# Local attention and a gated MLP on one core: two heads' logits in one matmul, q and k in a ring, and a new order of the work

## The chip, the core and the metric

One Trainium2 chip, one of its cores. The metric is device time in microseconds, the median of a few runs. The core has a matrix engine (TensorE, PE in the profile), a vector engine (VectorE, DVE), an activation engine (ScalarE, ACT), a general engine (GpSimd, POOL) and a queue that issues transfers (SyncE, SP). They run side by side and wait for each other with semaphores. Matrix products go to PSUM, eight banks of 512 fp32 columns on 128 partitions. ACT and DVE carry them from there to SBUF.

## The reference, cut to what matters

```python
B, S, D = 1, 2048, 448; H = 16; Dh = 28; W, dil = 8, 2; Fh = 896
def _A_ref(x, wqkv, wo):                       # dilated local attention
    q, k, v = split_heads(x @ wqkv)
    idx = pos[:, None] - (arange(W) * dil)[None, :]     # the keys s, s-2, ..., s-14
    logits = einsum('bhsd,bhswd->bhsw', q, k[idx]) * Dh ** -0.5
    attn = softmax(where(idx >= 0, logits, -1e9))
    return einsum('bhsw,bhswd->bhsd', attn, v[idx]) @ wo
def _B_ref(x, w_in, w_sp, b_sp, w_out):        # gated MLP that mixes tokens
    z = gelu(x @ w_in); z1 = z[..., :Fh]; z2 = layernorm(z[..., Fh:])
    g = einsum('ts,bsf->btf', w_sp, z2) + b_sp[None, :, None]
    return (z1 * g) @ w_out
h = x + _A_ref(layernorm(x), ...); out = h + _B_ref(layernorm(h), ...)
```

Everything is bf16 in and out, 2048 tokens of 448 channels.

## The kernel before

**Stages.** Each of the 16 tiles of 128 tokens is loaded to x_tm. DVE makes its statistics (L625, L627), POOL the root (L619, L620), and DVE the normalized tile xn (L636). It is transposed to xhT: tiles 0 to 3 on PE with an identity (L665, copied out by ACT), the others by a DMA transpose (dma_T). From xhT PE makes q and k (jobs qk, five parts of tokens in the list QT, four groups of four heads each), with heads padded from 28 to 32 rows in the weights wqk, and v (jobs v, two blocks at a time). Attention runs over 18 blocks of queries (GEOM: 128, then 112 or 114 tokens, with 14 or 16 earlier keys). For a block PE makes the logits of 16 heads (jobs lg, L785), ACT the exponentials E (L797, L798), DVE sets all but the eight wanted keys to zero (L807), PE multiplies with v (jobs oA and oB, L820; a column of ones gives the sums), and DVE divides (L837, L840) into otm. A DMA transposes otm to OT, in some blocks by way of OTs and a copy (oc). PE projects 256 tokens with wo (jobs y), DVE adds x (L749) and the second layer norm follows, transposed to hnT. Then come the two halves of z (L496 again: z2 with a layer norm, z1), the mixing product with w_sp (L949), the gate (L958, L961), the last projection (L973), the sum (L980) and the stores. The line L506 is a helper for copies and L496 one for products in two halves A and B; their tiles tell the jobs apart.

**Tiles of the array.** Products with L496 and L820 use 64 rows by 128 columns of the array, two side by side. The logits of a block use 28 rows by 64 columns: 32 matmuls of 64 columns, in two jobs of 16, lg0 for partitions 0 to 63 and lg1 for 64 to 127. The second waits until the first has ended, and another job stands between them.

**Order.** Every piece of work is a job with what it reads and writes. ORDER is a list of all jobs' numbers, written out, that sets the order on each engine's queue; the number of the job "warm" in it places filler matmuls. BANK lists the PSUM bank of each ticket (a piece of PSUM that a product holds until it is carried out), and ON the engine for jobs that can run on ACT, DVE or POOL. Each queue is served in order. SP issues all loads, transposes and stores.

**Memory.** qkT holds q and k of all 2048 tokens; the upper half of w_sp (wsp_hi) comes into the same place later. V1 and E lie where the lower half's second part (wsp_lb) comes later.

Of the kernel before, what the change touches and what calls it, by code (L numbers as in the profile page):

```python
# [1048 lines left out]
```

## Time and profile before

| what | value |
|---|---|
| median of three runs | 246.53 us (243.91 to 248.43) |
| the profiled execution | 245.12 us |
| its span, first to last instruction | 243.4 us |
| mean granted clock of TensorE | 0.993 |
| PE, DVE, ACT, POOL busy | 96%, 60%, 34%, 14% of the span |

The span in slices shows three parts. Up to some 23 us data arrive and the first products start. Up to some 122 us attention, projections and z run mixed, with all engines in use. From there to 230 us PE runs the mixing product and the last projection alone, and some 13 us of tail follow. Times in rows of the timeline are microseconds from the span's start; a row gives start, busy time, engine, line, operation, tiles and, in brackets, how long the engine stood idle before it and for whom.

### The profile page before, as it was taken

Reading aid. Unit: us, or ns where it says so; the run is one execution under the profiler, and the core shown is the slowest. Engines: PE = TensorE matmul, PEld = TensorE weight load, DVE = VectorE, ACT = ScalarE, POOL = GpSimd, SP = SyncE. Lnnn points to the kernel's source line nnn. Section 1 sums busy time; section 2 is a strip of 40 time slices with the busy share of each in tenths; the row PEclk is TensorE's granted clock in tenths of the full one; section 3 lists DMA queues with packets and bytes.
Section 4 is the critical chain, followed back from the end, with each engine's and each line's share of the span. In section 5 each row is a group of like instructions: output and inputs, shape, how many; then the busy total and the mean of one; then the engine's idle time right before and its main releaser. Section 6 shows DMA issues by size and latency. Waiting matters only on the chain.

```text
span 243.4 us, 6131 instructions
## 1 busy us (share of the span) xinstructions
PE 233.3 (96%) x2688; PEld 120.4 (49%) x2688; DVE 146.5 (60%) x327; ACT 81.8 (34%) x99; POOL 33.4 (14%) x79
## 2 busy tenths in 40 slices
PE   7997997999999899999999999999999999999995
PEld 2674553556555455555544444444444444444443
DVE  7889862999788798898875014047313042633474
ACT  3778374372977259767740000000000000000000
POOL 6454020022121111231331000000000000000000
PEclk9999997999999999999999999999999999999999
DMA  6955757366488875859999940000000000012012
GB/s 207 345 167 112 107 108 142 90 99 159 88 135 88 116 130 107 108 119 196 203 179 238 198 84 3 0 0 0 3 19 0 0 0 4 0 38 95 21 38 94
DMA packets 66315, 23.34 MB, mean 96 GB/s; under 512 B 58608, under 2 KB 66160, under 8 KB 66288
## 3 DMA queue, kind: packets, MB, share of 16 engines
q1 hardware_dynamic: 66288, 22.95, 46.9%
q8 instruction: 21, 0.34, 0.6%
q14 instruction: 6, 0.05, 0.1%
HBM read 6.83 MB, written 1.84 MB: 36 GB/s over the span
## 4 chain that ended last, share of the span: by engine, by line
PE 78%; DVE 9%; DMA 7%; ACT 2%; issue 1%; POOL 1%; SPq 1%; POOLq 0%
PE psum L949 38%; PE psum L496 28%; PE psum L973 8%; DVE st L625 2%; DMA x_tm<-in_A_x_dram 2%; PE psum L820 2%; DMA OT<-otm 2%; DMA OTs<-otm 2%; DMA xhT<-xn 2%; DVE E L807 1%; DVE xn L636 1%; DVE ub L958 1%; ACT qkT L506 1%; DVE mv L627 1%; POOL rs L620 1%
## 5 line engine op out<-in xcount | busy, mean ns | idle before, releaser
L958 DVE TENSOR_TENSOR ub<-psum,bb 128x512 bf16<-128x512 f32 x28 | 19.3, 691 | 56.5 <-PE psum L949 56.0
L949 PE MATMUL psum<-wsp_hi,z2p 128*128 128x512 bf16 x224 | 50.3, 379 | 0.0
L949 PEld LDWEIGHTS psum<-wsp_hi,z2p 128*128 128x128 bf16 x224 | 21.9, 98 | 26.1 <-DVE ub L958 0.4
L496 PE MATMUL psum<-xhT,wqk 64*128 64x512 bf16 (+1 forms) x280 | 29.1, 339 | 0.7 <-DMA xhT<-xn 0.7
L949 PE MATMUL psum<-wsp_lb,z2p 128*128 128x512 bf16 x112 | 26.3, 379 | 0.0
L949 PE MATMUL psum<-wsp_la,z2p 128*128 128x512 bf16 x112 | 25.8, 379 | 0.0
L496 PE MATMUL psum<-w_in,hnT 64*128 64x448 bf16 x224 | 25.0, 349 | 0.0
L496 PE MATMUL psum<-hnT,w_in 64*128 64x512 bf16 x196 | 24.1, 376 | 0.0
L973 PE MATMUL psum<-w_out,z1p 128*128 128x448 bf16 (+1 forms) x119 | 22.7, 342 | 0.4 <-DVE z1p L961 0.4
L506 ACT ACTIVATE qkT<-psum 128x1024 bf16<-128x1024 f32 (+1 forms) x18 | 15.3, 859 | 16.1 <-PE psum L496 16.1
L625 DVE BATCH_NORM_STATS2 st<-x_tm 128x6 f32<-128x448 bf16 x32 | 19.5, 610 | 0.6 <-DMA x_tm<-in_A_x_dram 0.4
L884 DVE BATCH_NORM_STATS2 st<-z2p 128x6 f32<-128x448 bf16 x32 | 19.0, 610 | 1.2 <-ACT z2p L877 1.0
L798 ACT ACTIVATE E<-psum 128x1024 bf16<-128x1024 f32 x17 | 16.6, 1028 | 4.0 <-PE psum L785 3.8
L980 DVE TENSOR_TENSOR srg<-psum,x_tm 128x448 bf16<-128x448 f32 (+1 forms) x17 | 9.8, 593 | 13.0 <-PE psum L973 11.0
L949 PEld LDWEIGHTS psum<-wsp_lb,z2p 128*128 128x128 bf16 x112 | 11.0, 98 | 13.2
L949 PEld LDWEIGHTS psum<-wsp_la,z2p 128*128 128x128 bf16 x112 | 10.9, 98 | 13.3 <-DVE z2p L893 0.4
L496 PEld LDWEIGHTS psum<-xhT,wqk 64*128 64x128 bf16 x280 | 13.2, 95 | 8.5 <-issue 0.9
L620 POOL TENSOR_TENSOR rs<-rs,negh 128x2 f32<-128x2 f32 (+2 forms) x22 | 17.1, 776 | 1.8
L973 PEld LDWEIGHTS psum<-w_out,z1p 128*128 128x128 bf16 x119 | 11.5, 98 | 10.9 <-DVE z1p L961 0.9
L496 PE MATMUL psum<-wo,OT 64*128 64x448 bf16 x112 | 14.2, 367 | 2.5 <-DMA OT<-otm 1.8
L820 PEld LDWEIGHTS psum<-V,E 64*128 64x128 bf16 x576 | 12.3, 93 | 8.6 <-DVE E L807 1.9
L496 PEld LDWEIGHTS psum<-w_in,hnT 64*128 64x128 bf16 x224 | 11.3, 94 | 9.6 <-ACT OT L506 0.2
(61 smaller groups left out, 233.9 us busy)
## 6 DMA issues: line engine op xcount, KB each, us to landing
w_in<-in_B_w_in_dram SPq DMA_DIRECT2D x8, 224.0 KB, 3.6
out_dram<-srg SPq DMA_DIRECT2D x16, 112.0 KB, 1.7
x_tm<-in_A_x_dram SPq DMA_DIRECT2D x3, 448.0 KB, 6.2
wraw<-in_A_wqkv_dram SPq DMA_DIRECT2D x2, 448.0 KB, 4.2
w_out<-in_B_w_out_dram SPq DMA_DIRECT2D x1, 784.0 KB, 5.3
bb<-in_B_b_sp_dram SPq DMA_DIRECT2D x1, 512.0 KB, 5.4
wv<-in_A_wqkv_dram SPq DMA_DIRECT2D x2, 224.0 KB, 6.5
wo<-in_A_wo_dram SPq DMA_DIRECT2D x1, 336.0 KB, 7.7
```

Source lines behind the costliest of these rows:

```text
L496: ins = e.matmul(out(k), w(k, p0, c), x(k, p0, c), start=(k, p0, c) in first, stop=(k, p0, c) in last, tile_position=(p0, 0))
L506: j = pl.job(name, eng, key, [(lambda e: e.activation(o(), i(), AF.Copy) if eng == "act" else e.tensor_copy(o(), i()), list(reads), list(w ...
L620: (lambda e: e.tensor_tensor(R, A, negh[:, 0:1].to_broadcast([128, n]), ALU.pow), [rr, r_negh], r_rs[k][m:m + n])],
L625: [(lambda e: e.bn_stats(st[:, m, :], src), [rsrc], [r_st[k][m]])], dve_t(D))
L627: [(lambda e: e.bn_aggr(mv[:, m, :], st[:, m, :]), [r_st[k][m]], [r_mv[k][m]])], 0.09)
L798: return e.activation(o[:, :, :, 0:64], psum[:, tk.b * 512:tk.b * 512 + 1024].rearrange("p (i h q) -> p i h q", i=2, q=64), AF.Exp, scale= ...
L820: ins = e.matmul(psum[:, c:c + DH + 1], E[64 * r:64 * r + 64, slot, a:a + 128], V1[64 * r:64 * r + 64, vs, 4 * (2 * k + gg) + hh, 0:DH + 1 ...
L884: [(lambda e, m=m, k=k: e.bn_stats(st3[:, m, k, :], z2p[:, m, D * k:D * (k + 1)]), [r_z2[m]], [r_st[2][m]])], dve_t(D))
L949: ins = e.matmul(psv(tk), z2p[:, s, 128 * fc:128 * fc + 128], w[:, 512 * (tc % 2):512 * (tc % 2) + 512], start=(s == 0), stop=(s == NB - 1))
L958: [(lambda e, tc=tc, s=s, tk=tk: e.tensor_tensor(ub[:, s, :], psv(tk), bb[:, 512 * tc:512 * tc + 512], ALU.add), [r_bb], [r_ub[s]])], dve_ ...
L973: ins = e.matmul(psv(tk, 0, c1 - c0), z1p[:, fc, 128 * m:128 * m + 128], w_out[:, fc, c0:c1], start=(fc == 0), stop=(fc == FC7 - 1))
L980: [(lambda e, m=m, s=s, tk=tk, c0=c0, c1=c1: e.tensor_tensor(srg[:, s, c0:c1], psv(tk, 0, c1 - c0), x_tm[:, m, c0:c1], ALU.add), [r_x[m]], ...
```

## The change

**Logits.** q is written twice, to qd: copy 0 holds the even heads of each group with the odd heads' rows zeroed, copy 1 the odd heads. k goes to kT alone. One matmul then takes 64 rows (two heads' k) against both copies of q, 2 x 64 columns, on 64x64 tiles of the array. A block has 16 such matmuls in one job, where it had 32 in two; block 0 keeps two jobs.

**Evacuation.** Where one pass carried q and k of a group out of PSUM, there are now a pass for k (job qe, L512) and the masked q (job qf): two passes on ACT with a column of zeros and ones as scale (L723), or on DVE one multiplication of double width (L726).

**Ring.** qd and kT hold 1592 tokens. The fifth part of q and k (tokens 1578 to 2047, 14 of them made a second time) is written over the first two parts, once the blocks that read those are done. The parts have other lengths: 256, 312, 512, 512, 470 columns. V1 lies elsewhere, and the masks are made for all partitions.

**Order.** ORDER, BANK and ON are new throughout. `'z2c3'`, `'z2c6'` and `'z2c7'` move from DVE to ACT, `'ve10'` as well.

```diff
-QT = [(0, 256), (256, 512), (512, 1024), (1024, 1536), (1536, 2048)]
+QT = [(0, 256), (256, 568), (568, 1080), (1080, 1592), (1578, 2048)]
...
-ORDER = [21, 44, 29, 27, 22, 25, 43, 30, 0, 45, 46, 1, 52, 28, 2, 120, 121, 53, 47, 48, 3, 23, 54, 55, 4, 122, 5, 6, 128, 124,
+ORDER = [21, 45, 22, 24, 0, 25, 1, 53, 2, 44, 54, 46, 47, 27, 3, 55, 121, 124, 23, 48, 131, 49, 56, 4, 59, 61, 926, 926, 926,
...
+            [("qd", [128, 4, 2, SL], BF16), ("kT", [128, 4, SL], BF16)],
...
+        pl.job("qmz", "dve", -58.5, [(lambda e: e.memset(qm[:], 0.0), [], [r_qm])] +
+               [(lambda e, p=p: e.memset(qm[p:p + 32, p // 32 % 2:p // 32 % 2 + 1], 1.0), [r_qm], [r_qm]) for p in (0, 32, 64, 96)], 0.35)
...
-                move("qe%d_%d" % (t, g), "act", lo / 112.0 + KEY["qe"] + KEY["qkg"] * g,
-                     lambda lo=lo, hi=hi, g=g: qkT[:, 2 * g:2 * g + 2, lo:hi],
...
+                move("qe%d_%d" % (t, g), "act", ekey, lambda n=n, a=a, g=g: kT[:, g, a:a + n], lambda n=n, tk=tk: psv(tk, 1, n),
+                     [], [r_qk[t][3 * g]] + [r_qk[o][3 * g] for o in also], evac_t(n), [tk], (tk, 1, 1))
...
+                def fa(e, i, n=n, a=a, g=g, tk=tk):
+                    return e.activation(qd[:, g, i, a:a + n], psv(tk, 0, n), AF.Copy, scale=qm[:, i:i + 1])
+
+                def fv(e, n=n, a=a, g=g, tk=tk):
+                    return e.tensor_tensor(qd[:, g, :, a:a + n], psv(tk, 0, n).unsqueeze(1).to_broadcast([128, 2, n]),
+                                           qm[:].unsqueeze(2).to_broadcast([128, 2, n]), ALU.mult)
...
-                    for g in range(4):
-                        for i in range(2):
-                            p = 32 * (2 * j + i)
-                            c = (tk.b + i) * 512 + (128 * g if b == 0 else 64 * (4 * j + g))
-                            for r in range(2):
-                                ins = e.matmul(psum[64 * r:64 * r + 64, c:c + wd], qkT[p:p + DH, 2 * g + 1, k0 + 64 * r:k0 + 64 * r + 64],
-                                               qkT[p:p + DH, 2 * g, t0 + u0 * r:t0 + u0 * r + wd], start=True, stop=True,
-                                               tile_position=(p, 64 * r))
+                    for g in gs:
+                        for r in range(2):
+                            c0 = (tk.b + r) * 512 + 2 * ps_ * (g - gs[0])
+                            for c in range(2):
+                                o = psum[64 * c:64 * c + 64, c0:c0 + 2 * ps_].rearrange("p (s q) -> p s q", s=2)[:, :, 0:wd]
+                                ins = e.matmul(o, kT[64 * r:64 * r + 64, g, ks + 64 * c:ks + 64 * c + 64],
+                                               qd[64 * r:64 * r + 64, g, :, qs + u0 * c:qs + u0 * c + wd], start=True, stop=True,
+                                               tile_position=(64 * r, 64 * c))
```

Three places of the new order. First PE ahead of the first output projection (`wo,OT`; `xhT,wqk` is q and k, `qkT` are logits, `V_82,E` one half of a block's outputs). Before, from the second half of block 2's outputs on:

```order
L820 MATMUL psum<-V_82,E 128x29 x16
L496 MATMUL psum<-xhT,wqk 128x512 x6
L785 MATMUL psum<-qkT 64x64 x64
L496 MATMUL psum<-xhT,wqk 128x512 x8
L820 MATMUL psum<-V_82,E 128x29 x16
L496 MATMUL psum<-xhT,wqk 128x512 x6
L820 MATMUL psum<-V_82,E 128x29 x16
L496 MATMUL psum<-xhT,wqk 128x512 x8
L785 MATMUL psum<-qkT 64x64 x64
L496 MATMUL psum<-wo,OT 128x448 x8
```

After, the last ten rows ahead of the projection, and its first (`qd,kT` are logits, `wv,xhT` is v; block 2's outputs lie nine rows further up):

```order
L502 MATMUL psum<-xhT,wqk 128x512 x8
L814 MATMUL psum<-qd,kT 64x128 x16
L502 MATMUL psum<-xhT,wqk 128x512 x14
L845 MATMUL psum<-V_81,E 128x29 x16
L502 MATMUL psum<-xhT,wqk 128x512 x6
L845 MATMUL psum<-V_81,E 128x29 x16
L502 MATMUL psum<-wv,xhT 128x448 x8
L845 MATMUL psum<-V_81,E 128x29 x16
L502 MATMUL psum<-wv,xhT 128x448 x6
L845 MATMUL psum<-V_81,E 128x29 x16
L502 MATMUL psum<-wo,OT 128x448 x8
```

Between block 2's outputs and the projection stood 28 q/k matmuls, 128 of logits and two halves of outputs; now 56, 64 wider ones, 14 of v and six halves. The logits of a block now stand alone, so PE goes to them 19 times where it went 8 times.

Second, ACT at the start (`wqk` are pieces of padded weights, `xhT` the copies of a transposed tile). Before:

```order
L506 ACTIVATE wqk<-wraw 128x2x8x28
L506 ACTIVATE xhT<-psum 128x2x128 x2
L506 ACTIVATE wqk<-wraw 128x2x4x28
L506 ACTIVATE xhT<-psum 128x4x128
L506 ACTIVATE wqk<-wraw 128x2x4x28
L506 ACTIVATE wqk<-wraw 128x2x8x28 x2
L506 ACTIVATE qkT<-psum 128x2x256 x2
```

After:

```order
L512 ACTIVATE wqk<-wraw 128x2x8x28 x2
L512 ACTIVATE wqk<-wraw 128x2x4x28 x2
L512 ACTIVATE wqk<-wraw 128x2x8x28
L512 ACTIVATE xhT<-psum 128x2x128 x2
L512 ACTIVATE xhT<-psum 128x4x128
L512 ACTIVATE wqk<-wraw 128x2x4x28
L512 ACTIVATE kT<-psum 128x256
L723 ACTIVATE qd<-psum,qm 128x256 x2
```

The first copy of xhT has moved from behind one piece of weights to behind five, and a group's one copy has become three passes.

Third, DVE where the tiles 2 and 3 are normalized (`xn`). Before, behind the statistics of tiles 2, 3 and 4:

```order
L625 BN_STATS st_62<-x_tm 128x6
L627 BN_AGGR mv_63<-st_62 128x2
L625 BN_STATS st_62<-x_tm 128x6
L636 TENSOR_SCALAR xn<-x_tm,mv_63,rs_68 128x512 x2
L625 BN_STATS st_62<-x_tm 128x6 x2
```

After, the same place, behind the statistics of tiles 2 to 8:

```order
L634 BN_STATS st_62<-x_tm 128x6
L636 BN_AGGR mv_63<-st_62 128x2
L645 TENSOR_SCALAR xn<-x_tm,mv_63,rs_68 128x512
L634 BN_STATS st_62<-x_tm 128x6
L645 TENSOR_SCALAR xn<-x_tm,mv_63,rs_68 128x512 x3
```

The xn of tiles 2 and 3 have moved behind the statistics of four more tiles.

More of the change, by code (lines that the diff above doesn't have):

```diff
@@ L405, in bass_sequential_preLN__sliding_local_dilated__mixer_gmlp__prompt_kernel @@
         negh = sb("negh", [128, 1], F32)
+        qm = sb("qm", [128, 2], F32)
         tscr = sb("tscr", [128, 2], F32)
@@ L411, in bass_sequential_preLN__sliding_local_dilated__mixer_gmlp__prompt_kernel @@
         NV = 6
-        (qkT, o_qk), (wsp_hi, o_wh) = region(
-            [("qkT", [128, 8, S_TOK], BF16)],
+        SL = 1592
+        (qd, o_qk), (kT, _), (wsp_hi, o_wh) = region(
+            [("qd", [128, 4, 2, SL], BF16), ("kT", [128, 4, SL], BF16)],
             [("wsp_hi", [128, NB, 1024], BF16)])
-        (wv, o_wv), (xhT, o_xh), (wqk, o_wp), (z1p, o_z1), (w_out, o_wout) = region(
-            [("wv", [128, 4, D], BF16), ("xhT", [128, 4, S_TOK], BF16), ("wqk", [128, 4, 8, 128], BF16)],
+        (wv, o_wv), (xhT, o_xh), (wqk, o_wp), (V1, o_v), (z1p, o_z1), (w_out, o_wout) = region(
+            [("wv", [128, 4, D], BF16), ("xhT", [128, 4, S_TOK], BF16), ("wqk", [128, 4, 8, 128], BF16), ("V1", [128, NV, NHEAD, 32], BF16)],
             [("z1p", [128, FC7, S_TOK], BF16), ("w_out", [128, FC7, D], BF16)])
-        (E, o_e), (V1, o_v), (wsp_lb, o_wl) = region(
-            [("E", [128, NE, ESL], BF16), ("V1", [128, NV, NHEAD, 32], BF16)],
+        (E, o_e), (wsp_lb, o_wl) = region(
+            [("E", [128, NE, ESL], BF16)],
             [("wsp_lb", [128, 8, 1024], BF16)])
@@ L431, in bass_sequential_preLN__sliding_local_dilated__mixer_gmlp__prompt_kernel @@
         r_xh = [[spot("xh%d_%d" % (m, i), o_xh, 4 * S_TOK * 2) for i in range(XEH.get(m, 1))] for m in range(NB)]
-        r_qk = [[spot("qk%d_%d" % (t, g), o_qk, 8 * S_TOK * 2) for g in range(4)] for t in range(len(QT))]
+        r_qk = [[spot("qk%d_%d" % (t, g), o_qk, 12 * SL * 2) for g in range(12)] for t in range(len(QT))]
         r_E = [spot("E%d" % i, o_e + i * ESL * 2, ESL * 2) for i in range(NE)]
@@ L693, in bass_sequential_preLN__sliding_local_dilated__mixer_gmlp__prompt_kernel, with make_qk @@
                      [W_qk[i]], [r_pad[(i, k, g)] for g in range(g0, g1)], {"act": 0.052 + n / 1200.0, "dve": 0.068 + n / 3840.0})
-        for t, (lo, hi) in enumerate(QT):
-            n = hi - lo
+        def make_qk(t, also=()):
+            lo, hi = QT[t]
+            n, a = hi - lo, lo if t < 4 else 0
             for g in range(4):
@@ L705, in bass_sequential_preLN__sliding_local_dilated__mixer_gmlp__prompt_kernel @@
                         lambda k, p0, c, lo=lo, hi=hi: xhT[p0:p0 + 64, c, lo:hi], n, tk, lambda part, rd=rd: rd)
-                move("qe%d_%d" % (t, g), "act", lo / 112.0 + KEY["qe"] + KEY["qkg"] * g,
-                     lambda lo=lo, hi=hi, g=g: qkT[:, 2 * g:2 * g + 2, lo:hi],
-                     lambda n=n, tk=tk: psum[:, tk.b * 512:tk.b * 512 + 1024].rearrange("p (k t) -> p k t", k=2)[:, :, 0:n],
-                     [], [r_qk[t][g]], evac_t(2 * n), [tk], tk)
+                ekey = lo / 112.0 + KEY["qe"] + KEY["qkg"] * g
+                move("qe%d_%d" % (t, g), "act", ekey, lambda n=n, a=a, g=g: kT[:, g, a:a + n], lambda n=n, tk=tk: psv(tk, 1, n),
+                     [], [r_qk[t][3 * g]] + [r_qk[o][3 * g] for o in also], evac_t(n), [tk], (tk, 1, 1))
+                name = "qf%d_%d" % (t, g)
+                eng = ON.get(name, "act")
+                def fa(e, i, n=n, a=a, g=g, tk=tk):
[3 more added lines that the diff above has]
+                                           qm[:].unsqueeze(2).to_broadcast([128, 2, n]), ALU.mult)
+                wr = [[r_qk[o][3 * g + 1 + i] for o in (t,) + tuple(also)] for i in range(2)]
+                ops = [(lambda e, i=i, fa=fa: fa(e, i), [r_qm], wr[i]) for i in range(2)] if eng == "act" else [(fv, [r_qm], wr[0] + wr[1])]
+                durs = {"act": 2 * act_t(n), "dve": dve_t(2 * n)}
+                j = pl.job(name, eng, ekey, ops, durs[eng], use=[tk], rel=(tk, 0, 1))
+                j.alts = durs
+        for t in range(4):
+            make_qk(t)
         o_jobs = {}
@@ L768, in bass_sequential_preLN__sliding_local_dilated__mixer_gmlp__prompt_kernel @@
             slot = b % NE
+            if b == 6:
+                make_qk(4, (0, 1))
             rq = []
             for t, (lo, hi) in enumerate(QT):
-                if lo < t0 + nq and hi > t0 - pad:
+                if (t == 4 if b >= 14 else t < 4 and lo < t0 + nq and hi > t0 - pad):
                     rq += r_qk[t]
@@ L774, in bass_sequential_preLN__sliding_local_dilated__mixer_gmlp__prompt_kernel, with f @@
             var = {0: 0, 16: 1, 14: 2}[pad]
[L775 to L787 removed]
+            off = 1578 if b >= 14 else 0
+            for j in range(2 if b == 0 else 1):
+                tk = Ticket(2)
+                gs = (2 * j, 2 * j + 1) if b == 0 else range(4)
+                def f(e, qs=t0 - off, ks=t0 - pad - off, gs=gs, ps_=128 if b == 0 else 64, tk=tk, wd=wd, u0=u0):
+                    for g in gs:
[6 more added lines that the diff above has]
+                                               tile_position=(64 * r, 64 * c))
                     return ins
                 lgs[(b, j)] = pl.job("lg%d_%d" % (b, j), "pe", b + KEY["lg"], [(f, rq, [])], 0.2, acq=tk, kind="L")
[L790 to L791 removed]
                 def f2(e, j=j, slot=slot, tk=tk, b=b):
@@ L801, in bass_sequential_preLN__sliding_local_dilated__mixer_gmlp__prompt_kernel @@
                                       act_t(8 * 78 if b == 0 else 1024), use=[tk], rel=tk, tbl="exp")
-            if b:
-                pl.apart.append((lgs[(b, 0)], lgs[(b, 1)]))
             def fm(e, slot=slot, wd=wd, var=var):
```

38 lines of the change are left out of this document (16 added, 22 removed), and 89 rows, old and new, of tables (BANK, ON, ORDER).

## The prediction

> **What bounds the kernel now.** I read the page first (busy time, the 40 slices), then the stretches, then the chain of waits and TensorE's timeline where it stood still.
>
> ```profile
> PE 233.3 (96%) x2688; PEld 120.4 (49%) x2688; DVE 146.5 (60%) x327; ACT 81.8 (34%) x99; POOL 33.4 (14%) x79
> PE   7997997999999899999999999999999999999995
> DVE  7889862999788798898875014047313042633474
> ACT  3778374372977259767740000000000000000000
> ```
>
> TensorE (PE) is busy for 96% of the span. VectorE (DVE) and ScalarE (ACT) are busy only in the first half. So whatever takes work or waits from PE counts one for one; work added to the other engines counts where PE comes to wait for it.
>
> ```profile
> 12.00:23.00 11.00, 9.29 (x246) 6.13 (x242) 9.85 (x28) 9.33 (x14) 5.86 (x14) 1.00 0.53 137
> 23.00:38.00 15.00, 13.34 (x332) 7.84 (x332) 10.87 (x27) 8.62 (x10) 1.90 (x3) 1.00 0.67 112
> 35.40:38.80 3.40, 1.61 (x74) 1.16 (x72) 1.92 (x5) 2.28 (x3) 0.63 (x1) 1.00 0.62 87
> 38.80:42.20 3.40, 3.40 (x36) 1.69 (x32) 0.02 (x1) 1.02 (x1) 0.00 (x0) 0.50 0.87 186
> 42.20:62.00 19.80, 19.80 (x484) 11.61 (x482) 18.08 (x41) 9.81 (x10) 3.13 (x7) 1.00 0.57 113
> 62.00:83.00 21.00, 19.94 (x545) 11.74 (x545) 16.50 (x39) 15.16 (x17) 3.70 (x7) 1.00 0.72 104
> 83.00:122.00 39.00, 39.00 (x402) 20.73 (x398) 35.06 (x82) 28.43 (x33) 8.97 (x19) 1.00 0.82 143
> 122.00:230.00 108.00, 108.00 (x512) 49.88 (x511) 38.68 (x74) 2.33 (x3) 3.06 (x6) 1.00 0.24 49
> ```
>
> The columns are the stretch, its length, busy time of PE, PE's weight loads, DVE, ACT and POOL, then the granted clock. From 83 to 230 us PE has no idle time at all, and the change leaves those matrix products alone. Everything it can win or lose lies before 83 us and in the tail. There PE waits 1.7 us before 23, 1.7 us before 38, 1.1 us between 62 and 83, and it runs at half clock from 38.8 to 42.2, which wastes 3.4 x 0.5 = 1.7 us.
>
> The profiled execution took 245.12 us, 1.7 more than its span of 243.4. The median of the runs shown, 246.53, is 1.4 above it. My sum is made against 245.1.
>
> **1. The logits on PE: 0.0, between -3.8 and +4.3.**
>
> ```profile
> 28.51 0.82 PE L496 MATMUL psum<-xhT,wqk 64*128 64x512 bf16 x6
> 29.16 0.37 PE L820 MATMUL psum<-V,E 64*128 64x29 bf16 x16
> 29.36 1.69 PE L496 MATMUL psum<-xhT,wqk 64*128 64x512 bf16 x14
> ...
> 31.11 0.82 PE L496 MATMUL psum<-xhT,wqk 64*128 64x512 bf16 x6
> 31.86 0.87 PE L785 MATMUL psum<-qkT 28*64 28x64 bf16 x64
> 32.66 1.04 PE L496 MATMUL psum<-xhT,wqk 64*128 64x512 bf16 x8
> ```
>
> The first number is the start, so starts are compared. Six products take 0.65 us when the next work has the same 64x128 tiles (28.51 to 29.16) and 0.75 when logits follow (31.11 to 31.86): the way into the logits' tiles costs 0.10. The 64 logits of two blocks take 0.80 with the way back. Before: 18 blocks at 0.40 is 7.2, and PE goes into the logits 8 times, 0.8: together 8.0 us.
>
> After, a block is 16 matmuls of 128 columns in four quarters of the array, in place of 32 of 64 columns.
>
> ```profile
> 31.93:31.96 0.03, 0.03 (x12) 1.00 0.21 25
> 31.96:32.00 0.03, 0.03 (x16) 1.00 0.14 17
> ```
>
> These stretches of 0.032 us, of the logits alone, see 12 and 16 matmuls in flight, four more each time: four run side by side in 0.032. Six 512-column products take 0.65, two side by side, so a column costs 0.65/3/512 = 0.42 ns, and 64 more columns lengthen a group of four to 0.059. A block is four groups, 0.24; 18 make 4.3 us. But the new order goes into the logits 19 times. At 0.10 in and, as I assume, as much out, that is 3.8, and the total 8.1. What the wider matmul saves, the way in and out takes back. No row shows 64x64 tiles. If changing to them were free, the term is -3.8; if only two of the four ran side by side, +4.3. I take the nearest row, the 32x64 tiles that the kernel has, for both. The 14 tokens computed twice cost 28 pairs x 14 columns x 0.42 ns = 0.2.
>
> [...]
>
> **2. The start: +1.0.** The rows are the page's on DMA issues (the last number is us to landing) and the timelines of PE, ACT and DVE.
>
> ```profile
> xhT<-xn SPq DMA_TRANSPOSE x12, 3.5
> ...
> 8.04 2.90 PE L496 MATMUL psum<-xhT,wqk 64*128 64x256 bf16 x50
> ...
> 23.16 1.04 PE L496 MATMUL psum<-xhT,wqk 64*128 64x512 bf16 x8 [0.66 <-DMA xhT<-xn]
> 5.64 0.58 ACT L506 ACTIVATE wqk<-wraw 128x448 bf16<-128x448 bf16 x1 [3.36 <-DMA wraw<-in_A_wqkv_dram]
> 6.13 0.64 ACT L506 ACTIVATE xhT<-psum 128x256 bf16<-128x256 f32 x2
> 10.37 0.81 DVE L636 TENSOR_SCALAR xn<-x_tm,mv,rs 128x512 bf16<-128x512 bf16 x2 [0.28 <-POOL rs L620]
> 15.81 0.61 DVE L625 BATCH_NORM_STATS2 st<-x_tm 128x6 f32<-128x448 bf16 x1
> 16.46 0.18 DVE L627 BATCH_NORM_AGGREGATE mv<-st 128x2 f32<-128x6 f32 x1
> 16.56 0.60 DVE L625 BATCH_NORM_STATS2 st<-x_tm 128x6 f32<-128x448 bf16 x1
> ```
>
> Now ACT makes one piece of the padded weights ahead of the first copy of xhT; after, five, some 2 us of them (about 0.5 for a large one, 0.3 for a half), so I put the first product near 9.2 instead of 8.04. DVE now normalizes tiles 2 and 3 at 10.37; after, four more pairs of statistics stand ahead, 0.75 each (15.81 to 16.56), and adding them up I get 13.4 (an estimate, like the times that follow). ACT's order has the copies of those tiles ahead of the last k and q of the first 256 tokens, so block 0's logits come at about 16.7. PE meanwhile lacks work. The product of the third part of q and k needs one more transpose (tile 8); its xn comes near 20.6, and with 3.5 us to land PE starts it near 24.4 instead of 23.16. It then lacks two blocks of logits (0.6), and has 56 more tokens (0.65) and half a block of outputs (0.2). Net +1.0; I take 0 to +2.
>
> **3. The first output projection: -3.5.**
>
> ```profile
> 35.58 0.93 PE L785 MATMUL psum<-qkT 28*64 28x64 bf16 x64
> 38.30 1.24 PE L496 MATMUL psum<-wo,OT 64*128 64x448 bf16 x8 [1.79 <-DMA OT<-otm]
> 33.80 4.36 DMA OT<-otm
> ```
>
> The last row is from the chain: the transpose takes 4.36 us to land. PE waits 1.79 us for the transposed outputs of block 2, and the half clock follows. From the second half of block 2's outputs PE now has 28 q/k products (3.0 us), 128 logits (1.6) and two halves of outputs (0.4, by 29.16 to 29.36), some 5.1, ahead of the projection; it needed 7.2 (31.11 to 38.30). After, it has 56 (6.0), 14 v products (1.3), four blocks of logits (1.7) and six halves (1.2), 10.2. The wait should go, with the 1.7 us of half clock behind it. Late next would be the transposes for the fourth part of q and k: tile 12 is issued behind three loads of w_in, and I see about 1 us of room.
>
> **4. Evacuations: +1.5.**
>
> ```profile
> L506 ACT ACTIVATE qkT<-psum 128x1024 bf16<-128x1024 f32 x11 | 11.2, 1025 | 13.7 <-PE psum L496 13.7
> L506 ACT ACTIVATE qkT<-psum 128x512 bf16<-128x512 f32 x7 | 4.2, 599 | 2.4 <-PE psum L496 2.4
> L506 ACT ACTIVATE xhT<-psum 128x256 bf16<-128x256 f32 x2 | 0.6, 372 | 0.0
> L506 DVE CAST qkT<-psum 128x1024 bf16<-128x1024 f32 x1 | 1.2, 1225 | 0.1
> L506 DVE CAST qkT<-psum 128x512 bf16<-128x512 f32 x1 | 0.7, 686 | 0.0
> ```
>
> One pass per group becomes a k pass and, on ACT, two masked q passes. ACT now spends 11.2 + 4.2 = 15.4 us on them. After: 12 passes of 256 columns (372 ns), 10 of 312 (some 420), 15 of 512 (599) and 11 of 470 (some 560), 23.8 us. With one v evacuation taken from DVE, ACT gains 9.3 us before 75 us. DVE gains three double q passes (1225 each) and six k passes, 7.3, and loses 3.0. A masked ACT pass has no row; I take the copy's time, and 0.05 more on 34 passes would be 1.7 us of ACT. ACT has the room: in the stretches shown above from 12 to 83 us it was busy 42.9 of 66.8 us. But a group's three passes (3 x 0.6) now last longer than its 14 products (14 x 0.107 = 1.5), so PE may wait for a bank between 24 and 42 us: +0.5, estimated. Between 42 and 70 the same DVE work falls into a shorter time; it was already busy 18.1 of 19.8 us: +1.0 on top of the 1.1 us of waits there. Without ACT's room the price would be up to the 9.3. From 83 to 122 ACT takes three copies of z2 from DVE, under 3.1 us by the 1024-column row, hidden: it was busy 28.4 of 39.
>
> **5. The tail: -0.5.**
>
> ```profile
> 233.37 1.49 PE L973 MATMUL psum<-w_out,z1p 128*128 128x448 bf16 x7
> 234.80 0.42 DVE L961 TENSOR_TENSOR z1p<-ub,z1p 128x512 bf16<-128x512 bf16 x1
> 235.28 5.49 PE L973 MATMUL psum<-w_out,z1p 128*128 128x448 bf16 x35 [0.42 <-DVE z1p L961]
> ```
>
> Seven matmuls now stand between the last gate product and a wait for DVE's last z1p. After, 13 stand there, 1.1 us more cover.
>
> **Sum:** 0.0 + 0.2 + 1.0 - 3.5 + 1.5 - 0.5 = -1.3, so 245.1 - 1.3 = 243.8 us.
>
> **The rivals.**
> - *The clock halves early.* In the stretch before the half clock PE was busy 1.61 of 3.40 us; with the new start I count about 1.4 of 3.4 between 13.5 and 16.9. Another 1.7 us would go: 245.5. Against it: PE then waits less at tile 8. [...]
> - *The wait moves instead of going.* The SP queue is served in order, and its transposes wait for xn and otm. If the fourth q/k part or the projection still waits as long, term 3 is lost: 245.1 + 2.2 = 247.3.
> - *ACT sets the pace* (slower). If between 20 and 70 us PE finds the banks of q unread each time, ACT's added 9.3 us come through and hide the old waits (-3.5): 245.1 + 9.3 - 3.5 = 250.9. It decides once ACT's waits for PE's q and k, 13.7 + 2.4 us now, fall below some 4. For it: a group's passes outlast its products. Against: v, logits and outputs stand between the products.
> - *Visits to the 64x64 tiles are cheap.* Then 243.8 - 3.8 = 240.0.
> - *The 64x64 tiles run two at a time:* the wider matmul saves nothing and the visits cost: 243.8 + 4.3 = 248.1.
>
> **Chances.** Forecast 0.36, clock 0.14, moved wait 0.14, ACT 0.12, cheap visits 0.20, two at a time 0.04. Two per cent (4.9 us) is about what a measurement can tell from no change. Against the median shown, faster by that means below 241.6: the cheap visits and some of the forecast's spread, 0.24. Slower means above 251.5: most of the ACT case and its spread, 0.11. Within: 0.65. The range is 239.5 (cheap visits) to 249.5, which leaves out the ACT case and the far ends.
>
> **What would show it.** Logits: starts of a block's 16 matmuls 0.06 apart by fours, some 0.1 lost at each end. Start: first q/k product after 9 us, PE idle between 13 and 17. Projection: no wait for OT, and clock 1.00 at 38 to 45. Evacuations: PE's waits for qd and kT under 2 us in all. I am wrong if the half clock stays, or if ACT's wait for PE nearly disappears.

## The result, and the profile after

| | time, median of the runs | against the kernel before, 95% interval |
|---|---|---|
| before, beside the changed kernel | 245.95 us (243.91 to 248.43, 15 runs) | |
| changed kernel | 243.02 us (241.62 to 244.48, 15 runs) | 0.9893 (0.9865 to 0.9920) |
| before, beside the second series | 245.19 us (242.53 to 248.59, 29 runs) | |
| changed kernel, a second series | 243.02 us (241.60 to 243.83, 12 runs) | 0.9933 (0.9900 to 0.9966) |

The ratios are of fast runs alone (a run over 1.5% above the fastest of its kernel is left out), so they are not quite the quotients of the medians. The change takes off 0.7 to 1.1%, less than the 2% that the prediction takes for the mark, but both intervals lie below 1. The profiled execution took 243.01 us, its span 241.3. It is compared with the 245.12 and 243.4 of before: -2.1 us.

The page of the changed kernel, busy time and slices:

```profile
PE 233.5 (97%) x2397; PEld 116.4 (48%) x2408; DVE 145.7 (60%) x332; ACT 93.8 (39%) x132; POOL 35.6 (15%) x83
PE   7869999999999999999999999999999999999995
ACT  3697898588876797797630000000000000000000
PEclk9997999999999999999999999999999999999999
```

TensorE (PE) is as busy as before with 291 recorded matmuls fewer. ScalarE (ACT) has 12 us more work, all in the first half. The low digit of the clock stands in the fourth slice, near 20 us; before it stood near 40. The stretches say more (length, then busy time of PE, weight loads, DVE, ACT and POOL, then the granted clock):

```profile
12.00:23.00 11.00, 9.03 (x120) 4.80 (x118) 9.54 (x28) 8.72 (x18) 5.16 (x14) 0.84 0.45 99
15.37:18.78 3.41, 1.67 (x30) 0.65 (x26) 3.41 (x11) 3.41 (x7) 1.50 (x4) 1.00 0.34 61
18.78:22.19 3.41, 3.41 (x44) 1.57 (x38) 2.87 (x9) 2.53 (x4) 1.70 (x7) 0.50 0.51 95
23.00:38.00 15.00, 15.00 (x288) 8.27 (x284) 10.14 (x22) 13.21 (x23) 2.60 (x5) 1.00 0.85 146
38.00:62.00 24.00, 24.00 (x546) 13.44 (x544) 21.67 (x48) 18.93 (x27) 4.36 (x8) 1.00 0.66 109
62.00:83.00 21.00, 21.00 (x440) 11.76 (x438) 18.04 (x44) 15.53 (x19) 3.56 (x9) 1.00 0.88 136
```

From 23 to 83 us PE has no idle time left. It had 1.7 us before 38 and 1.1 us between 62 and 83, and 3.4 us at half clock behind the first output projection. Now the half clock comes at 18.78, behind a stretch in which PE was busy for 1.67 of 3.41 us. The timelines of DVE and PE show the start, the first output projection and the tail:

```profile
6.89 0.80 DVE L512 COPY wqk<-wraw 128x448 bf16<-128x448 bf16 x1 [0.66 <-DMA wraw<-in_A_wqkv_dram]
7.61 0.72 DVE L645 TENSOR_SCALAR xn<-x_tm,mv,rs 128x512 bf16<-128x512 bf16 x2
...
10.07 1.81 PE L502 MATMUL psum<-xhT,wqk 64*128 64x256 bf16 x30
17.45 0.33 PE L814 MATMUL psum<-qd,kT 64*64 64x156 bf16 x8 [1.75 <-ACT qd L723]
27.00 1.90 PE L502 MATMUL psum<-xhT,wqk 64*128 64x512 bf16 x16
28.84 0.42 PE L814 MATMUL psum<-qd,kT 64*64 64x128 bf16 x16
29.19 1.69 PE L502 MATMUL psum<-xhT,wqk 64*128 64x512 bf16 x14
...
44.93 0.92 PE L502 MATMUL psum<-wo,OT 64*128 64x448 bf16 x8
...
230.56 8.13 PE L998 MATMUL psum<-w_out,z1p 128*128 128x448 bf16 x49
```

The account of the profiled execution. The third part of q and k starts at 27.00 instead of 23.16, 3.8 later; about 0.25 of that is work (56 more tokens and half a block of outputs, two blocks of logits fewer, by the prediction's prices), 1.7 the half clock, and 1.9 the late first product and the wait at 17.45. Behind it 4.9 us are won by the start of the mixing product (120.84 instead of 122.10): the wait of 1.79 for OT, the 1.7 us of half clock behind it, and 1.4 of others, of which the smaller waits between 62 and 83 us are 1.1. From there to the end another 0.8 goes: the last 49 matmuls run through, where a wait of 0.42 stood before; the other 0.4 isn't traced. 3.6 - 4.9 - 0.8 = -2.1.

The half clock is not in every execution. Of the first 15 runs of the changed kernel 11 show a mean clock of 0.99 (median 243.15) and 4 one of 1.00 (242.02). Of 29 runs of the kernel before, in the second series, 9 show 1.00 (244.0) and 11 show 0.992 or 0.993 (245.7), the rest others. At one clock or the other the changed kernel is ahead by 2 to 2.6 us, so the gain doesn't hang on it.

### The profile page after: what moved, and what is told of

Same layout as the page of the kernel before. It is cut to its first block, busy times and chain, and to the rows that moved or that the text cites. A ratio compares the mean times of both kernels' runs of the same rounds, so it can differ in the third digit from the quotient of the medians.

```text
span 241.3 us, 5610 instructions
## 1 busy us (share of the span) xinstructions
PE 233.5 (97%) x2397; PEld 116.4 (48%) x2408; DVE 145.7 (60%) x332; ACT 93.8 (39%) x132; POOL 35.6 (15%) x83
## 4 chain that ended last, share of the span: by engine, by line
PE 79%; DVE 13%; POOL 2%; DMA 2%; ACT 1%; issue 1%; SPq 1%; DVEq 0%
PE psum L974 40%; PE psum L502 25%; PE psum L998 9%; DVE st L909 5%; PE psum L845 3%; PE psum L814 3%; DVE st L634 3%; DMA wraw<-in_A_wqkv_dram 2%; POOL rs L629 1%; DVE xn L645 1%; DVE z2p L918 1%; DVE x_tm L775 1%; DVE mv L912 1%; DVE mv L636 1%; POOL rs L628 1%
## 5 line engine op out<-in xcount | busy, mean ns | idle before, releaser
L502 PE MATMUL psum<-xhT,wqk 64*128 64x512 bf16 (+3 forms) x280 | 29.4, 342 | 0.0
L502 PE MATMUL psum<-w_in,hnT 64*128 64x448 bf16 x224 | 24.7, 349 | 0.1
L502 PE MATMUL psum<-hnT,w_in 64*128 64x512 bf16 x196 | 24.3, 376 | 0.0
L825 ACT ACTIVATE E<-psum 128x1024 bf16<-128x1024 f32 x17 | 17.3, 1023 | 5.1 <-PE psum L814 4.8
L723 ACT ACTIVATE qd<-psum,qm 128x512 bf16<-128x512 f32 (+3 forms) x34 | 18.2, 592 | 1.8 <-PE psum L502 1.8
L502 PEld LDWEIGHTS psum<-xhT,wqk 64*128 64x128 bf16 x280 | 12.4, 96 | 8.7 <-DVE wqk L512 0.5
L502 PEld LDWEIGHTS psum<-w_in,hnT 64*128 64x128 bf16 x224 | 10.6, 94 | 10.7 <-DVE x_tm L775 0.6
L628 POOL TENSOR_SCALAR rs<-mv 128x2 f32<-128x2 f32 (+2 forms) x22 | 6.7, 303 | 60.4 <-DVE mv L636 41.0
L946 ACT ACTIVATE z1p<-psum 128x1024 bf16<-128x1024 f32 x14 | 14.0, 1020 | 4.1 <-PE psum L502 4.0
```

What stands on the lines that cost most here:

```text
L502: ins = e.matmul(out(k), w(k, p0, c), x(k, p0, c), start=(k, p0, c) in first, stop=(k, p0, c) in last, tile_position=(p0, 0))
L628: [(lambda e: e.tensor_single_scalar(A, mv[:, m:m + n, 1], EPS, ALU.add), r_mv[k][m:m + n], [rr]), (lambda e: e.tensor_tensor(R, A, negh[: ...
L723: return e.activation(qd[:, g, i, a:a + n], psv(tk, 0, n), AF.Copy, scale=qm[:, i:i + 1])
L825: return e.activation(o[:, :, :, 0:64], psum[:, tk.b * 512:tk.b * 512 + 1024].rearrange("p (i h q) -> p i h q", i=2, q=64), AF.Exp, scale= ...
L946: return e.activation(o, i, AF.Gelu_apprx_tanh)
```

## The experiments

The starts of some pieces of PE's work, in us, from the profiled execution of each kernel (the mixing product marks the end of the part that differs):

| kernel | first q/k | first logits | third part of q/k | first projection | projection at 60 | mixing | mean clock |
|---|---|---|---|---|---|---|---|
| changed | 10.07 | 17.45 | 27.00 | 44.93 | 60.45 | 120.84 | 0.993 |
| changed, again | 10.26 | 17.65 | 25.88 | 43.79 | 59.32 | 119.42 | 1.00 |
| narrow | 10.09 | 17.47 | 25.71 | 43.91 | 61.10 | 122.99 | 1.00 |
| narrow, again | 10.17 | 17.56 | 27.29 | 46.51 | 63.43 | 124.29 | 0.993 |
| narrow, shifted | 10.06 | 17.45 | 26.96 | 45.02 | 60.70 | 121.18 | 0.993 |
| flat | 10.15 | 17.53 | 26.94 | 43.83 | 58.33 | 118.24 | 0.993 |
| more ACT | 10.08 | 18.69 | 29.84 | 49.62 | 66.07 | 127.09 | 0.993 |
| start, first trial | 9.12 | 18.53 | 28.03 | 45.95 | 61.48 | 121.69 | 0.993 |
| start, second | 9.07 | 15.10 | 26.39 | 44.84 | 60.37 | 121.30 | 1.00 |
| start, third | 7.87 | 15.55 | 27.78 | 45.68 | 61.21 | 121.36 | 1.00 |
| q on DVE | 10.04 | 16.79 | 25.60 | 43.51 | 59.03 | 119.14 | 1.00 |

My theory behind the result was that the new order brings the gain and the width next to nothing. The rival: the width brings it.

**The width alone.** Three runs with narrow logits in the new order (narrow, narrow shifted, narrow again in the table).

```diff
-  for r in range(2):
-      for c in range(2): matmul(both copies of q, 2 x 64 columns)
+  for s in range(2):              # one copy of q each
+      for r in range(2):
+          for c in range(2): matmul(copy s of q, 64 columns)
```

> The changed kernel with each wide logits matmul cut into its two copies of q: a block has 32 matmuls of 64 columns on the same 64x64 tiles, in the same place of the same order; nothing else differs. Theory (the gain comes from the new order, the width brings next to nothing): a group of four now starts every 0.056 us and should start every 0.032, so a block grows from 4 x 0.056 = 0.226 to 8 x 0.032 = 0.256, 18 blocks by 0.5 us: 243.0 + 0.5 = 243.5, about 0.990 of before. Rival (the 2.9 us gained come from the wider matmul and the 291 matmuls fewer): the time goes back to that of before, 245.9, ratio 1.00. Half of it back (244.5) would mean that both count.

Measured: 246.11 us, 1.0015 of before (0.9971 to 1.0059). The gain is gone, as the rival said, and yet the table does not show a wider matmul's time: from the third part to the first projection the cut kernel loses 0.3 us against the changed kernel at the same clock (0.17 ahead of it at the one, 0.12 behind at the other). By the projection at 60 it has lost 1.8, 1.5 of that at two places of its timeline:

```profile
53.16 0.29 PE L815 MATMUL psum<-qd,kT 64*64 64x64 bf16 x13 [0.42 <-issue]
57.44 0.19 PE L815 MATMUL psum<-qd,kT 64*64 64x64 bf16 x1 [0.71 <-issue]
```

PE stops inside a block's logits, after 19 and after 31 of its 32 matmuls, and waits for nothing that the profile shows. Numbered from 0 in order of start (PE's recorded matmuls, weight loads and semaphore instructions together), it resumes at records 1985 and 2241, 256 apart. The timeline of the kernel before has such a stop at record 2753, three times 256 further:

```profile
66.56 0.23 PE L820 MATMUL psum<-V,E 64*128 64x29 bf16 x5 [0.20 <-issue]
```

The trace also has transfers of instructions in pieces of 16,384 bytes, 21 in this kernel. So I suspected PE's own code. The next two runs tell that apart from a bank or an operand.

```diff
-  filler: matmul of 512 columns
+  filler: 4 matmuls of 128 columns        # the code behind it lies 138 records later
```

> The kernel with each wide logits matmul cut in two (32 of 64 columns), with one more edit: a filler matmul of 512 columns is now four of 128, so TensorE's instructions after the start lie 138 further on (69 matmuls, each with a weight load), for the same filler time. In the cut kernel TensorE stood still for 0.61 and 0.90 us inside two blocks' logits with nothing to wait for, at its recorded instructions 1985 and 2241, exactly 256 apart; in the kernel before 0.37 us at number 2753, three times 256 further; and the profile has TensorE's code come in pieces of 16 KB, the next ready some 1.5 us after its transfer ends. Theory (the code comes too late where 256 instructions last under some 4.3 us): the stalls again sit at numbers 193 + 256k, but now at other matmuls; none at those two blocks, and likeliest where 256 instructions take under 4 us: near 36 and 69 us. Rival (a bank or an operand of those two blocks): the same two blocks stall by 0.6 and 0.9 again, at numbers 138 higher. Time in both cases 244 to 246.5.

> The kernel with each wide logits matmul cut in two, once more, nothing altered. If TensorE's stalls inside two blocks' logits come from its code arriving in pieces of 256 instructions, they come back at recorded instructions 1985 and 2241 (blocks 9 and 10 of the attention, 0.3 to 0.9 us), since the program is the same, and the median is again 1 to 1.5 us above that of the shifted program (244.8): 245.5 to 246.5. If they were a chance of one execution, no stall and 244 to 245.

Measured, shifted: 244.81 us, 1.0006 (0.9968 to 1.0044). The two blocks run through; no gap at any record 193 + 256k exceeds 0.2 us. That refutes the rival, but no other matmul stalls either, so the guess on where was wrong. Measured, repeated: 245.37 us, 1.0053 (1.0014 to 1.0093), so 0.6 us above the shifted kernel, not the 1 to 1.5 expected, with both stops back in the same places, the third at record 1217, where the first run had only 0.34 between two starts, and a fourth near record 3009 (PE's timeline):

```profile
41.01 0.82 PE L502 MATMUL psum<-xhT,wqk 64*128 64x512 bf16 x6 [0.99 <-issue]
55.76 0.29 PE L815 MATMUL psum<-qd,kT 64*64 64x64 bf16 x13 [0.42 <-issue]
59.76 0.19 PE L815 MATMUL psum<-qd,kT 64*64 64x64 bf16 x1 [0.43 <-issue]
74.16 0.93 PE L502 MATMUL psum<-w_in,hnT 64*128 64x448 bf16 x8 [0.34 <-issue]
```

The transfers beside the stops, from the trace's records of the instruction queue (us):

```
kernel          record  last 256 records took* piece transferred   PE resumed   behind the transfer
before            2753                   3.21   64.06 to 65.05          66.56                  1.51
narrow            1985                   5.95   49.95 to 51.63          53.16                  1.53
narrow            2241                   4.28   54.94 to 55.88          57.44                  1.56
narrow, again     1217                   5.85   38.12 to 39.06          41.01                  1.95
narrow, again     1985                   5.95   53.40 to 54.36          55.76                  1.40
narrow, again     2241                   4.00   57.46 to 58.49          59.76                  1.27
```

(* the stop included.) PE resumes 1.3 to 2.0 us behind the end of a transfer each time. The pieces at 49.95, 53.40 and 38.12 started 2.75, 3.6 and 3.0 us after the boundary ahead of them, those at 57.46 and 54.94 started 1.7 and 1.8 us after theirs. In the shifted kernel the pieces between 33 and 60 us started 0.1 to 1.4 us after theirs. In the kernel before it was 0.7, but there 256 records lasted only 3.2 us. In these rows a stop comes where a piece starts late, or where the code is used up very fast. Why a piece starts late isn't shown. The changed kernel, with 32 records per block of logits in place of 64, has no such stop in either profile. So my theory stands in the records, where the width's own time is 0.3 us, and falls in the median: without the wide matmul the new order is level with the kernel before, or a little behind, in all three runs.

What the stops cost can be read from the table. From the third part to the projection at 60 us the shifted kernel takes 33.7 us, the other two 35.4 and 36.1, so the stops take 1.7 and 2.4 us there. They do not explain the whole. The shifted kernel has none, and its median is still 1.8 us behind the changed kernel of the same series (244.81 against 243.02). And the intervals of the three ratios overlap, so a cost of the stops in the median isn't shown. Nor was a narrow kernel with an order of its own run: this order belongs to the wide logits, and what loses may be the pair of the two.

**The way into the logits' tiles** (flat).

```diff
-  16 matmuls: 64 keys x (2 x 64 queries) on 64x64 tiles, for both halves of the keys
+   8 matmuls: 128 keys x (2 x 64 queries) on 64x128 tiles
```

> The changed kernel with the logits on 64x128 tiles, the tiles of the products around them: a matmul takes all 128 keys of a block against the first half's queries, 8 matmuls a block in place of 16. The logits of the upper 64 keys are thereby those of other queries, so this attention isn't the reference's; all shapes and all other work stay. Theory (the way into and out of the 64x64 tiles costs 0.09 to 0.10 us each): 19 visits x 0.19 = 3.6 us go, 243.0 - 3.6 = 239.4, and six products followed by logits take 0.65 us instead of 0.75. If PE only waits more elsewhere instead, less. Rival (the tiles' change is free, and the 0.1 is the read of q or the first matmul's own time): no change, 243.0.

Measured: 239.87 us, 0.9806 (0.9753 to 0.9859). Five of its six runs have a clock of 1.00; at that clock it is 2.1 us ahead of the changed kernel (239.73 against 241.80), so about 1 us of the 3.15 between the medians is the half clock that comes less often here. A visit that took from 28.84 to 29.19 takes 0.23:

```profile
28.66 0.40 PE L813 MATMUL psum<-qd,kT 64*128 64x128 bf16 x8
28.89 1.69 PE L502 MATMUL psum<-xhT,wqk 64*128 64x512 bf16 x14
```

Matched piece by piece, ACT's work is 0.07 us ahead of the changed kernel at 27 us and 3.05 ahead at 75. Between them lie 16 visits, so one costs 0.19 (the 0.17 in the next expectation shares the 3.05 among 18). At the mixing product 2.6 are left, since a wait of 0.50 us for OT at 86 us takes some back, and 2.0 at the end of the span (239.3 against 241.3). The theory holds for the price of a visit; of the 3.6 us that it expected, some 2 arrive.

**Fewer visits.** Then merging three of the 19 should bring 0.5.

```diff
-  lg5  qk3_0B  lg4   ...  lg10  v10B y2A lg11 y2B  lg9   ...  lg16  y6B v16A  lg15
+  lg5  lg4  qk3_0B   ...  lg10  lg9  v10B y2A lg11 y2B   ...  lg16  lg15  y6B v16A
```

> The changed kernel with three of its 19 visits to the logits' tiles merged: the logits of block 4 come directly behind those of block 5, of block 9 behind block 10, of block 15 behind block 16 (and ACT's exponentials of 9 ahead of those of 11); no other work moves. Theory (a visit costs 0.17 us in and out, by the flat trial's 3.05 us for 18): 0.5 us less by 72 us, unless a bank is not free in time; about 242.5 at the end. Rival (the entry's 0.1 hides the first operands' read and merging frees nothing, or the merged logits wait for banks): 243.0 or more.

Measured: 245.05 us, 0.9974 (0.9937 to 1.0011). The rival: the logits that come earlier wait for DVE to empty their bank, 2.1 us in all, which costs more than the 0.5.

```profile
53.31 0.42 PE L774 MATMUL psum<-qd,kT 64*64 64x128 bf16 x16 [1.29 <-DVE otm L825]
69.80 0.42 PE L774 MATMUL psum<-qd,kT 64*64 64x128 bf16 x16 [0.79 <-DVE otm L825]
```

**The projection's wait alone, in the kernel before.**

```diff
-  lg7  y0A  qk3_3B  o4A  y0B  v6A  o4B  v6B      ACT: ex7  ex6
+  lg7  qk3_3B  v6A  y0A  o4A  y0B  o4B  v6B      ACT: ex6  ex7
```

> The kernel before with its first output projection put later in the order: the other half of a q/k product and the first half of a v product now stand ahead of it (some 1.5 us of products), and block 6's exponentials ahead of block 7's so that the v product's bank is free; the rest of the order and the narrow logits stay. Theory (order): the wait of 1.79 us for the transposed outputs shrinks to about 0.4 and the half clock behind it (1.7 us) goes, -2 to -3.1: 242.8 to 243.9, so the time of the changed kernel without its wide logits. Rival (the wait only moves to the next projection or to v, or the clock halves anyway): 245.9, no change.

Measured: 244.55 us, 0.9983 (0.9947 to 1.0020). Inside the trace the term is there: this execution started 1.21 us late (its weights landed later), and DVE's work is 1.21 behind that of before at 35 us and 1.25 ahead at 47, so 2.5 us were won, within the 2 to 3.1 expected. Then the second projection waits, since DVE makes the evacuation of v ahead of it:

```profile
39.45 0.92 PE L457 MATMUL psum<-wo,OT 64*128 64x448 bf16 x8
...
47.73 0.93 PE L457 MATMUL psum<-wo,OT 64*128 64x448 bf16 x8 [0.83 <-DVE V L467]
```

By 56 us it is 0.5 ahead, by the mixing 0.4. The half clock went (9 of 12 runs at 1.00 against 9 of 29), the rest was given back. An order gains as a whole: one wait alone gave only a part.

**ACT's room** (more ACT).

```diff
-  ops = [masked pass i for i in range(2)]      # on ACT
+  ops = [masked pass i for i in (0, 0, 1)]
```

> The changed kernel with the first masked pass of every group whose q is on ACT made twice (same source, same place, same values): 15 or so more passes of 256 to 512 columns, some 8 us of ACT, all between 11 and 66 us. Theory (ACT is covered: its waits for PE's q and k are still 4.8 us in all, and PE doesn't wait for banks behind 24 us): at most +1.5, most of it at the first logits, which wait for ACT's q (one more pass on each of four groups ahead of them, up to 1.5 us). Rival (ACT sets the pace): the 8 us come through, less the 4.8 of waits, +3 or more: 246 or more.

Measured: 249.59 us, 1.0227 (1.0179 to 1.0275): the rival. The 17 added passes are 9.9 us of ACT, and 6.6 of them come through. The groups of the page, first of this kernel, then of the changed one (instructions, busy us, mean ns):

```profile
L723 ACT ACTIVATE qd<-psum,qm 128x512 bf16<-128x512 f32 (+3 forms) x51 | 28.1, 588 | 1.4 <-PE psum L502 0.7
```

```profile
L723 ACT ACTIVATE qd<-psum,qm 128x512 bf16<-128x512 f32 (+3 forms) x34 | 18.2, 592 | 1.8 <-PE psum L502 1.8
```

PE's timeline in this kernel, and ACT's waits for q and k in the changed one (us in all, times, longest):

```profile
18.69 0.33 PE L814 MATMUL psum<-qd,kT 64*64 64x156 bf16 x8 [2.87 <-ACT qd L723]
29.04 0.37 PE L845 MATMUL psum<-V,E 64*128 64x29 bf16 x16 [0.42 <-ACT qd L723]
66.07 0.93 PE L502 MATMUL psum<-wo,OT 64*128 64x448 bf16 x8 [0.61 <-ACT qd L723]
```

```profile
ACT kT L512 <- PE psum L502: 3.0, 5, 1.6
ACT qd L723 <- PE psum L502: 1.8, 4, 1.0
```

1.2 us are lost at the first logits and the rest bit by bit up to 72 us. ACT's waits for q and k, 16.1 us before, are 4.8 in the changed kernel and 2.9 here. Of the 9.9 us added, 3.3 were absorbed: less than those 4.8, though ACT is idle for 61% of the span.

**The start.** Three trials, then one job. In the trials DVE normalizes tiles 0 and 1 ahead of the weights' copies, ACT gives up two to four weight pieces, and there are fewer fillers.

> The changed kernel with its start in another order: DVE normalizes tiles 0 and 1 ahead of the copies of weights that wait for their load, and tiles 2 and 3 ahead of most statistics of tiles 4 to 11; ACT copies xhT ahead of three weight pieces; two of ACT's weight pieces and one masked q go to DVE; fewer fillers. Everything after 25 us keeps its order. Theory (the start is a net loss of 3.6 us by the third part of q and k, 1.9 from the late first product and the wait for q, 1.7 from the half clock at 18.8): the first q/k product comes at 8.2 to 8.6 in place of 10.07, and PE has no stretch of 3.4 us that is half idle; the third part starts at 24 to 25.5, where the transpose of tile 8 (landed at 24.9) bounds it, in place of 27.0: 243.0 - 1.5 to 2.5 = 240.5 to 241.5. Rival (what is late at the start is hidden by later waits): no change, 243.0.

> The start in another order once more, mended: in the last trial DVE made the masked q of the last group, and had it at the end of a row of statistics; TensorE waited 4.2 us for it. Now DVE makes it directly behind the statistics of tile 7, and ACT carries k of that group ahead of the transposed tiles 2 and 3. Theory: first q/k product near 9.1 us as in the last trial (10.07 in the changed kernel), first logits near 15.5 in place of 17.45, no half clock behind, third part of q and k at 24.5 to 25.5 in place of 27.0; at the end -1 to -2.5 against the changed kernel, 240.5 to 242. Rival (later waits for transposes take it back): the third part starts earlier but the mixing product does not, 243.

> The changed kernel with its start put in order a third time. In the second trial TensorE's first logits came at 15.1 in place of 17.5, but it then waited 1.5 us for the transpose of tile 4, 1.3 for DVE to carry k out of the bank of the next v product, and a transfer was late at 88 us. Now: DVE takes two more weight pieces from ACT, a memset of E goes from DVE to POOL, tile 4 is normalized one statistic earlier, DVE carries the second part's k between statistics, and POOL makes no memset while DVE normalizes tile 0. Everything behind 25 us keeps its order. Theory (the start's loss can be recovered): first product near 8.0, first logits near 14, third part of q and k at 23.4 to 24.5 (27.0 with the half clock, 25.9 without, in the changed kernel), and what is gained there arrives at the mixing product: 118 to 119.4 against 120.8 and 119.4; 240.5 to 242. Rival (the transposes' queue sets the time between 60 and 95 us): third part early, mixing no earlier than 119.4 to 121; 242 to 243.5.

Measured: 244.15 (0.9981, 0.9946 to 1.0016), 243.76 (0.9963, 0.9927 to 0.9999) and 244.38 us (0.9959, 0.9921 to 0.9997). None is faster than the changed kernel. The first came to a wait of 4.2 us for the masked q, which I had put too late on DVE. All 12 runs of the second have a clock of 1.00, so there the half clock was avoided, and still it takes 2 us more than the changed kernel at that clock (241.8). In the second and third trial PE starts 1.0 and 2.2 us earlier and then waits; PE's timelines:

```profile
19.48 2.96 PE L462 MATMUL psum<-xhT,wqk 64*128 64x312 bf16 x42 [1.50 <-DMA xhT<-xn]
23.72 0.93 PE L462 MATMUL psum<-wv,xhT 64*128 64x448 bf16 x8 [1.28 <-DVE kT L472]
```

```profile
20.09 2.96 PE L462 MATMUL psum<-xhT,wqk 64*128 64x312 bf16 x42 [2.06 <-DMA xhT<-xn]
26.97 0.36 PE L805 MATMUL psum<-V,E 64*128 64x29 bf16 x16 [1.94 <-DVE E L792]
```

In the one for the transpose of tile 4, whose normalization stands behind DVE's statistics, and for DVE to empty k's bank; in the other for the same transpose and for the masked exponentials of block 0. In these trials DVE's order sets the pace up to 25 us, and a job pulled forward pushes back one that is needed as much. With an earlier first product alone nothing is won. So the last trial (q on DVE) moves one job into a place where DVE has time:

```diff
-  ACT: ... xe3 xe2 qe0_0 qf0_0 ve0 ...      DVE: ... n4 n5 st9 ...
+  ACT: ... xe3 xe2 qe0_0 ve0 ...            DVE: ... n4 n5 qf0_0 st9 ...
```

> The changed kernel with one job moved: DVE, not ACT, makes the masked q of the last group of the first part, one pass of double width between the normalization of tile 5 and the statistics of tile 9; nothing else is reordered. In the changed kernel TensorE waits 1.75 us for that job on ACT, and is busy for 1.67 of the 3.41 us in whose wake the clock halves. Theory (a smaller wait keeps that window more than half busy): first logits near 16.7 in place of 17.45, no half clock in nearly all runs, and DVE's later start of tile 8's statistics stays ahead of the queue that transposes them: 241 to 242, against 243.0. Rival (the transposes of tiles 4 and 8, or what the queue carries later, take it back as in the three trials of the start): clock 1.00 but 242.5 to 244.

Measured: 241.85 us (241.53 to 243.49), 0.9905 (0.9872 to 0.9937). All 12 runs have a clock of 1.00. The first logits in PE's timeline, and the stretch that was half idle in the changed kernel:

```profile
16.79 0.33 PE L774 MATMUL psum<-qd,kT 64*64 64x156 bf16 x8 [1.11 <-ACT kT L472]
```

```profile
15.37:18.78 3.41, 2.30 (x36) 0.87 (x32) 3.33 (x11) 3.15 (x6) 0.73 (x3) 1.00 0.38 77
```

The changed kernel's six runs at that clock, on the same chip, have a median of 241.80. So this order wins little by itself; it makes the better half of the runs the only one. By its absolute time it is ahead of both kernels; the intervals of the ratios overlap with those of the changed kernel. The second run of the changed kernel, which served as mark:

> The changed kernel once more, with nothing altered, beside the other runs of this series. Expected: about 0.989 of before, 243, and no stretch in which TensorE stands still inside a block's logits. It serves as the mark for the other three, and shows which details of the changed kernel's first profile come back: the half clock between 18 and 23 us, and no wait at any output projection.

The time came as expected (the ratio is 0.9933, not 0.989), and the details but for the half clock, which was absent from its profile and from 6 of its 12 runs.

## Why the prediction came out, point by point

**Forecast 243.8, measured 243.02;** -1.3 expected in the profiled execution, -2.1 found. The sum came near because errors of both signs met, so its nearness is in part luck.

1. **The logits, 0.0.** The size holds: a visit to the next start takes 0.35 us (28.84 to 29.19), groups of four start 0.056 apart (0.059 forecast), the way in costs 0.09, and by the flat trial in and out cost 0.19 together, where I took 0.20. All told some 8.2 us against the 8.0 of before. The rivals "cheap visits" and "two at a time" are refuted by these rows. What the term lacked is all that hangs on the width beside the logits' own time. Cut in two, they cost only 0.3 us more in the shifted kernel up to the mixing product, yet in the whole time the width is worth 1.8 to 3.1 us (244.81 to 246.11 against 243.02). In the profiles of the unshifted kernels the stops for code are 1.7 and 2.4 us of that. Beside them stand 1.65 us of late transfers between 95 and 101 us (narrow, the first two rows; PE waits there for DVE, which had waited 1.54 us for a transfer) and 0.67 us at a store's buffer in the tail (shifted, the third row):

   ```profile
   96.18 0.93 PE L502 MATMUL psum<-wo,OT 64*128 64x448 bf16 x8 [0.38 <-DVE OT L512]
   101.07 0.93 PE L502 MATMUL psum<-w_in,hnT 64*128 64x448 bf16 x8 [1.20 <-DVE x_tm L775]
   238.58 1.51 PE L999 MATMUL psum<-w_out,z1p 128*128 128x224 bf16 x14 [0.67 <-DVE srg L1006]
   ```

   In the shifted kernel a piece of code was transferred from 235.62 to 236.61 us, beside that last wait; the last piece of the other kernels here came between 225 and 230 us. Whether these waits follow from the width or from chance stays open, and so does the most of the shifted kernel's 1.8 us.
2. **The start, +1.0, measured +3.6.** The first product came at 10.07, not 9.2: I had counted ACT's weight pieces, not that DVE's piece waits for its load and that both xn stand behind it. And the rival "the clock halves early" came true, 1.7 us, in 11 of 15 runs. I had counted PE busy for 1.4 of 3.4 us there and set against it that PE waits less at tile 8, which lies behind that stretch. Without it the start was 1.9, within the 0 to +2.
3. **The first projection, -3.5.** Right: no wait for OT, full clock from 22 us on. The trial with the kernel before finds 2.5 of it for a part of the move, of which 0.4 are left at the mixing product.
4. **Evacuations, +1.5.** Wrong in sign: PE waits for no bank between 23 and 83 us, and the old waits of 1.1 us between 62 and 83 went too. I infer, and have not shown, that in the new order the next products find other banks free while a group's passes run. The masked passes, for which I took the copy's time, cost more: 688 ns at 512 columns in place of 599, and 18.2 us for all 34, some 1.4 more than counted (I had named 1.7 for that case). And the rival "ACT sets the pace" was nearer than 0.12 sounds: its point, ACT's waits below some 4 us, was missed by 0.8, and 9.9 us more on ACT cost 6.6.
5. **The tail, -0.5, measured -0.8.** Right as far as it is traced: more matmuls cover DVE's last products, and the wait of 0.42 is gone.

What I had named as the sign of an error, that the half clock stays, did come true, at another place.

## What to carry to other kernels

Count the instructions of the matrix engine as well as its time: here its code came late in places where 256 of them lasted 3.2 to 6.0 us, the stop included, and fewer, wider matmuls were worth more than their own time (1.8 to 3.1 us for 0.3), though the code explains only a part of it. Before moving work to an engine that looks 60% idle, see how long it waits for the engine that you want to keep busy; here that wait (4.8 us) was a far better guide to its room than the idle share. To mend a start, move one job into a real gap and look at what is late next, rather than pull everything forward.
